# Two decode attentions on one core: the output projection in four column groups of 128, with A's part and half of B's in a loop of matmuls into one row group

## The chip, the cores and the metric

One core of one Trainium2 chip. The metric is device time in microseconds, median over runs of one kernel. The profile is of one execution on the same core.

## The reference

Two independent attention blocks, A and B, each for a single query token with a cache of 8192 positions, 32 heads of 128. Each ends in an output projection by its own wo, and the two results stand side by side.

```python
def _A_ref(x, k_cache, v_cache, wq, wo):          # B is the same with its own tensors
    B, Sq, D = x.shape                            # 1, 1, 512
    H, Dh = 32, 128
    q = (x @ wq).reshape(B, Sq, H, Dh).transpose(0, 2, 1, 3)
    scores = jnp.einsum("bhqd,bhkd->bhqk", q, k_cache) * (Dh ** -0.5)   # 8192 keys a head
    p = softmax(scores, axis=-1)
    o = jnp.einsum("bhqk,bhkd->bhqd", p, v_cache)
    return o.transpose(0, 2, 1, 3).reshape(B, Sq, H * Dh) @ wo          # 4096 x 512
...
return jnp.concatenate([a, b], axis=-1)           # [1, 1, 1024], bf16
```

## The kernel before

**Tiling.** The 64 heads are worked through in N = 16 rounds of G = 4 heads. Each head has HP = 32 of the 128 partitions, and each partition holds T = 256 consecutive positions of its head. A round's K and V are 8 MB each. `kn` holds two rounds of K (two slots), `vn` one round of V.

**One round.** VectorE multiplies K by the query, broadcast along the positions (line 280, two halves). TensorE adds up the 128 products of each position by matmuls with the identity into `rps` (lines 432 to 438: a loop of NJ = 4 steps of four matmuls, whose address comes from the register `koff`), and VectorE finishes the sum (line 308). Lines 313, 315, 476 and 478 find the maximum of each head and spread it; ScalarE takes the exponentials and their sums (line 383). Line 484 sums the denominators over the partitions. Line 492 multiplies by V: 64 matmuls of 512 columns in four column groups, that is, four strips of 32 rows of the result `acc`, which the array can work on side by side. The If at line 489 waits, in the last two rounds, for the last quarter of V, which those rounds load by itself. In the next round VectorE's `part` (lines 285 to 292) adds up the pieces of `acc`, line 442 sums them over partitions, and line 297 divides by the denominator: four columns of `oD`, one for each head.

**Start.** wq of A and B come first into `vn`. Line 405 turns x on its side, and the loop at line 409 projects the queries: eight steps, each with an If (line 410) and eight matmuls of 512 columns (line 419), both of whose operands are addressed from registers. ScalarE copies the result into `qmem` (line 372). POOL's clears (lines 170 to 180, `o2` among them) must be done before TensorE's first matmul (line 402).

**End.** In the last round, once the round before is summed up (line 442), `mid` (lines 447 to 467) projects what is ready: all 32 heads of A and B's first 16. wo stands in `kn`, A's in the first half and B's in the second. The heads' outputs are first brought into wo's row order: VectorE spreads them with a mask (line 329), a matmul sums the spread pieces (line 450), and VectorE copies the result into `o2` (line 337). `o2[:, h, :]` has two columns for each head: the head's own vector, in column 0 for A and column 1 for B, and zeros. Line 452 clears the accumulator `yps[0]`, and line 461 then adds 48 products of 512 columns, head after head round the four column groups (`k = h % G * HP`), two rows in each. VectorE copies `yps[0]` to `yc` (line 348), and line 466 adds up the four groups' rows with a selector, in fp32, into two halves of 256 columns in `yps[1]`: rows 0 and 1 hold the first half for A and B, rows 32 and 33 the second.

Only then does TensorE go on to the last round's denominators (line 484) and V (line 492). Its queue keeps the program's order, so all of this waits behind `mid`. The 16 heads of B that are left follow in pieces of wo as they land (lines 497 to 509): two matmuls of 256 columns for each head, one to each half. Line 442 for the last four heads stands before the second piece; the last piece of heads waits for line 297's division (line 503). At the end VectorE and ScalarE copy a half each (lines 352 and 386), and ScalarE's queue stores two rows of 512.

**Queues.** All large loads go through SyncE's queue in the order written (lines 222 to 233). The last ones are A's wo and B's first 16 heads, the last round's V in two pieces, and B's other heads in six pieces. Small loads of x and the store are in ScalarE's queue.

Of the kernel before, what the change touches and what calls it, by code (L numbers as in the profile page):

```python
# [8 lines left out]
BF16 = mybir.dt.bfloat16  # L9
F32 = mybir.dt.float32  # L10

P = 128
# [33 lines left out]
def bass_concat_heads__mha_block_cached__gqa_block_cached__decode_kernel(  # L46
# [18 lines left out]
    NA = 2  # L65
    H, Sk, Dh = ks[0].shape[1:]
    D = xs[0].shape[2]
    NOUT = wos[0].shape[1]
# [4 lines left out]
    G = 4  # L73
    HP = P // G
# [15 lines left out]
    WOB = [(0, 16, True), (16, 4, True), (20, 4, True), (24, 4, True), (28, 2, False), (30, 1, False),  # L90
           (31, 1, False)]
    RG = [32, 16, 4]
    NH = NOUT // 2

    with ExitStack() as st:
        ec = st.enter_context
# [2 lines left out]
        def sb(name, shape, dt):  # L99
            return ec(nc.sbuf_tensor(name, shape, dt))  # L100

        KS = T * Dh
        kn = sb("kn", [P, 2 * KS], BF16)
# [4 lines left out]

        qmem = sb("qmem", [P, N * Dh // 2], F32)
        qflat = qmem[:].bitcast(BF16)  # L110
        yc = qmem[:, 0:NOUT]
        pt = sb("pt", [P, T + W, G], BF16)
        ptf = pt[:].rearrange("p t g -> p (t g)")
        s_sb = sb("s_sb", [P, T], F32)
# [3 lines left out]
        ones_bf = sb("ones_bf", [P, P], BF16)  # L118
        ones_f = sb("ones_f", [P, P], F32)
        zrow = sb("zrow", [1, P], BF16)  # L120
        ident = sb("ident", [P, P], BF16)
        ident_f = sb("ident_f", [P, P], F32)
        sel16 = sb("sel16", [P, W, G], F32)
# [6 lines left out]
        rinv = sb("rinv", [P, G], F32)  # L130
        oD = sb("oD", [P, G + NA * H], BF16)
        zb = sb("zb", [P, 2, P], BF16)
        o2 = sb("o2", [P, NA * H, NA], BF16)
        mask = {g: sb("mask%d" % g, [P, P // g], BF16) for g in RG}
        jsel = {g: sb("jsel%d" % g, [P, g], BF16) for g in RG}
        out_sb = sb("out_sb", [NA, NOUT], BF16)

        def ps(name, shape):
            return ec(nc.psum_tensor(name, shape, F32))
# [6 lines left out]
        yps = [ps("yps%d" % i, [P, 512]) for i in range(2)]  # L146
# [3 lines left out]
        def sem(name):  # L150
            return ec(nc.semaphore(name))

        s_x, s_woa, s_v, s_v2, s_out = (sem(n) for n in ("s_x", "s_woa", "s_v", "s_v2", "s_out"))
# [4 lines left out]
        c_pool, c_sel, c_mul, c_sr, c_g, c_gm, c_self, c_st, c_o, c_rl, c_yd = (  # L158
            sem(n) for n in ("c_pool", "c_sel", "c_mul", "c_sr", "c_g", "c_gm", "c_self", "c_st", "c_o", "c_rl", "c_yd"))

        c_qa, c_nb, c_p, c_ya = (sem(n) for n in ("c_qa", "c_nb", "c_p", "c_ya"))

        c_q, c_red, c_gx, c_bc, c_pv, c_ex, c_rm, c_y = (
            sem(n) for n in ("c_q", "c_red", "c_gx", "c_bc", "c_pv", "c_ex", "c_rm", "c_y"))

        RED = NB * NJ

        @block.gpsimd
        def _(e):
# [74 lines left out]
        def _(e):  # L244
            with once(e):
# [48 lines left out]
                def outs(dst):  # L294
                    w_self()
                    w_ex()
                    e.tensor_tensor(dst, mtp[:, EX:EX + G], rinv[:], ALU.mult).then_inc(c_o, 1)  # L297
# [36 lines left out]
                def lay(i):  # L334
                    a, h0, n = todo[i]
                    e.wait_ge(c_rm, i + 1)
                    e.tensor_copy(o2[:, a * H + h0:a * H + h0 + n, a],
                                  lay_ps[i][:, 0:n]).then_inc(c_rl, 1)


# [2 lines left out]
                for i in range(len(todo)):  # L343
                    lay(i)
                    if i + 2 < len(todo):
                        spread(i + 2)
                e.wait_ge(c_y, 1)
                e.tensor_copy(yc, yps[0][:]).then_inc(c_yd, 1)
                part()
                outs(o2[:, NA * H - G:NA * H, NA - 1])  # L350
                e.wait_ge(c_y, 2)
                e.tensor_copy(out_sb[:, 0:NH], yps[1][0:NA, 0:NH]).then_inc(c_yd, 1)  # L352


        @block.scalar
        def _(e):
            with once(e):
                for a in range(NA):
                    e.dma_start(xrow[a:a + 1, :], xs[a][0]).then_inc(s_x, 16)
                w_q = _Stepped(e, c_q, 1, 1)  # L360
                w_bc = _Stepped(e, c_bc, 1, 1)
                w_nb = _Stepped(e, c_nb, 1, 1)
                w_pv = _Stepped(e, c_pv, 1, 1)
                e.wait_ge(c_pv, 1)
                e.copy(xT[:].rearrange("p (a c) -> p c a", c=C),
                       misc[:, 0:C * NA].rearrange("p (c a) -> p c a", a=NA)).then_inc(c_qa, 2)
                with e.Fori(0, N // 2) as r:
                    for j in range(2):
                        w_q()
                        for h in range(G):  # L370
                            p = slice(h * HP, (h + 1) * HP)
                            i = e.copy(qflat[p, bass.ds(r * (2 * Dh) + j * Dh, Dh)],  # L372
                                       yps[j][p, h * Dh:(h + 1) * Dh])
                        i.then_inc(c_qa, 1)
                e.wait_ge(c_pool, NPOOL)
                with e.Fori(0, N):
                    w_bc()
                    e.activation(negb[:], bmp[:, 0:G], AF.Copy, scale=-scale).then_inc(c_nb, 1)  # L378
                    w_nb()
                    w_pv()  # L380
                    for h in range(G):
                        p = slice(h * HP, (h + 1) * HP)
                        e.activation(pt[p, 0:T, h], s_sb[p, :], AF.Exp, bias=negb[p, h:h + 1], scale=scale,  # L383
                                     accum_out=rsum[p, h:h + 1]).then_inc(c_p, 4)
                e.wait_ge(c_y, 2)
                e.copy(out_sb[:, NH:NOUT], yps[1][HP:HP + NA, 0:NH]).then_inc(c_ya, 1)
                e.wait_ge(c_yd, 2)
                e.wait_ge(c_ya, 1)
                e.dma_start(out[0].rearrange("o (a n) -> (o a) n", a=NA), out_sb[:]).then_inc(s_out, 16)


        @block.tensor
        def _(e):
            with once(e):
# [9 lines left out]
                for c in range(C):  # L404
                    i = e.matmul(misc[:, c * NA:(c + 1) * NA], xrow[:, c:D:C], ident[0:NA, 0:NA],
                                 start=True, stop=True)
                i.then_inc(c_pv, 1)
                e.wait_ge(s_w[0], 16)
                with e.Fori(0, N // 2) as r:
                    with e.If(r == GA // 2):  # L410
                        e.wait_ge(s_w[1], 16)
                    a = r // (GA // 2)
                    w0 = r * (2 * G * Dh) + a * (WQ - H * Dh)
                    x0 = a * C
                    for j in range(2):
                        e.wait_ge(c_qa, by_tile)
                        e.reg_add(by_tile, by_tile, 1)
                        for c in range(C):
                            i = e.matmul(  # L419
                                yps[j][:], xT[:, bass.ds(x0 + c, 1)].broadcast_to([P, P]),  # L420
                                vn[:, bass.ds(w0 + (c * H * Dh + j * G * Dh), G * Dh)],
                                start=(c == 0), stop=(c == C - 1))
# [21 lines left out]
                def wo_rows(h):  # L444
                    return kn[:, h * NOUT:(h + 1) * NOUT]

                def mid():
                    for i, (a, h0, n) in enumerate([(0, 0, H)] + [(1, h0, n) for h0, n, rows in WOB if rows]):
                        e.wait_ge(c_rl, (1, 2, 4, 6, 8)[i])
                        e.matmul(lay_ps[i][:, 0:n], zb[:, i % 2, :], jsel[n][:], start=True,  # L450
                                 stop=True).then_inc(c_rm, 1)
                    e.matmul(yps[0][:], zrow[:], ones_bf[0:1, 0:1].broadcast_to([1, 512]), start=True,
                             stop=False, skip_group_check=True)
                    e.wait_ge(c_rl, 5)
                    for h in range(H + WOB[0][1]):
                        if h == 0:
                            e.wait_ge(s_woa, 16)
                        if h == H:
                            e.wait_ge(s_wob[0], 16)
                        k = h % G * HP  # L460
                        i = e.matmul(yps[0][k:k + NA, :], o2[:, h, :], wo_rows(h), start=False,
                                     stop=False, skip_group_check=True)
                    i.then_inc(c_y, 1)
                    e.wait_ge(c_yd, 1)
                    for b in range(2):
                        e.matmul(yps[1][b * HP:b * HP + NA, 0:NH], sel16[:, 0, 0:NA],
                                 yc[:, b * NH:(b + 1) * NH], start=True, stop=False, skip_group_check=True)

                with e.Fori(0, N) as r:
                    with e.Fori(0, NB // 2):  # L470
# [16 lines left out]
                    for g in range(NG):  # L487
# [3 lines left out]
                        k = g % G * HP  # L491
# [5 lines left out]
                for g in range(1, len(WOB)):  # L497
                    h0, n, rows = WOB[g]
                    if g == 2:
                        total_of_group()  # L500
                    e.wait_ge(s_wob[g], 16)
                    if h0 == H - G:
                        e.wait_ge(c_o, N + 1)
                    for h in range(h0, h0 + n):
                        for b in range(2):
                            m = e.matmul(yps[1][b * HP:b * HP + NA, 0:NH], o2[:, H + h, :],  # L506
                                         wo_rows(H + h)[:, b * NH:(b + 1) * NH], start=False,
                                         stop=(h == H - 1), skip_group_check=True)
                m.then_inc(c_y, 1)

# [27 lines left out]
```

## Time and profile before

| what | value |
|---|---|
| runs before, median (lowest to highest) | 666.0 us (665.41 to 666.83) |
| the profiled execution's own time | 665.7 us |
| its span | 664.2 us |
| mean granted TensorE clock | 0.784 |
| TensorE matmuls busy | 385.1 us, 58% |
| VectorE busy | 363.3 us, 55% |
| ScalarE busy | 76.0 us, 11% |
| DMA | 285.22 MB, 429 GB/s over the span |

Times in views are microseconds from the span's start. "Busy" of an engine is the union of its instructions; an engine's idle time before an instruction is put down to what released it. A name with q (PEldq, SPq) is the sequencer of that engine: address arithmetic on registers, branches and DMA issues are seen there. In a line of a group or a source line, the three numbers of a duration are the lowest, the median and the highest in ns. In a view by windows the columns are the stretch and its length, then the busy time and count of TensorE's matmuls, its weight loads, VectorE, ScalarE and POOL, then the granted clock, the DMA's share and GB/s. The clock is a share of full speed: 0.50 is half.

### The profile page before, as it was taken

The numbers are of one execution on the slowest core, as the hardware profiler recorded it, in microseconds if no ns is written. First come the engines' busy times: TensorE is split into PE (matmuls) and PEld (weight loads), VectorE is DVE, ScalarE is ACT, GpSimd is POOL, SyncE is SP. The second block draws the span as 40 slices with busy tenths as digits, with TensorE's granted clock in tenths as the row PEclk, the third lists the DMA queues.
The fourth block names the chain that finished last, engine by engine and source line by source line (L and its number), as shares of the span: only waits on it lengthen the run. The fifth ranks groups of instructions, "written<-read, shape, count | busy, mean of one in ns | idle before, by whom it ended". The sixth has DMA issues, their size and how long they took to land.

```text
span 664.2 us, 7946 instructions
## 1 busy us (share of the span) xinstructions
PE 385.1 (58%) x2398; PEld 169.4 (25%) x2398; DVE 363.3 (55%) x250; ACT 76.0 (11%) x211; POOL 2.3 (0%) x12
## 2 busy tenths in 40 slices
PE   1719392854819275481928548192854819285776
PEld 0203141322304132230413223041322304132332
DVE  1046757548292654829275482927547292754821
ACT  1710202020010202001020200102020010202020
POOL 1000000000000000000000000000000000000000
PEclk9968787786958778695877869597786959778789
DMA  9999999999999999999989999999999999989998
GB/s 379 442 442 442 442 442 391 430 442 442 442 442 399 422 442 442 442 442 442 442 387 434 442 442 442 442 442 414 406 442 442 442 442 442 434 387 458 426 413 344
DMA packets 6472, 285.22 MB, mean 429 GB/s; under 512 B 708, under 2 KB 1224, under 8 KB 1608
## 3 DMA queue, kind: packets, MB, share of 16 engines
q1 hardware_dynamic: 6464, 285.22, 99.5%
q10 hardware_dynamic: 8, 0.00, 0.0%
HBM read 285.21 MB, written 0.00 MB: 429 GB/s over the span
## 4 chain that ended last, share of the span: by engine, by line
DMA 82%; PE 15%; issue 1%; ACT 1%; SPq 0%; ACTq 0%; DVE 0%
DMA vn<-in_A_v_cache_dram 41%; DMA vn<-in_B_v_cache_dram 34%; PE acc L492 13%; DMA kn<-in_B_wo_dram 5%; PE yps L419 2%; DMA vn<-in_A_wq_dram 2%; ACT qmem L372 1%; SPq L220 0%; PE yps L506 0%; SPq L208 0%; ACTq L43 0%; ACTq L372 0%; DVE out_sb L352 0%
## 5 line engine op out<-in xcount | busy, mean ns | idle before, releaser
L280 DVE TENSOR_TENSOR kn<-kn,qmem 128x16384 bf16<-128x16384 bf16 x32 | 276.7, 8688 | 49.6 <-DMA kn<-in_A_k_cache_dram 37.1
L436 PE MATMUL rps<-kn,ident 128*128 x1024 | 236.2, 383 | 0.4
L492 PE MATMUL acc<-vn,pt 128*32 128x512 bf16 x1024 | 92.0, 537 | 153.5 <-DMA vn<-in_A_v_cache_dram 80.4
L308 DVE TENSOR_REDUCE s_sb<-rps 128x64 f32<-128x512 f32 x64 | 44.3, 692 | 166.8 <-PE rps L436 166.8
L436 PEld LDWEIGHTS rps<-kn,ident 128*128 128x128 bf16 x1024 | 96.5, 98 | 110.4 <-issue 22.3
L492 PEld LDWEIGHTS acc<-vn,pt 128*32 128x32 bf16 x1024 | 38.4, 129 | 200.6 <-issue 194.3
L378 ACT ACTIVATE negb<-bmp 128x4 f32<-128x4 f32 x16 | 2.8, 173 | 547.3 <-PE bmp L478 547.3
L383 ACT ACTIVATE pt<-s_sb,negb 32x256 bf16<-32x256 f32 x64 | 54.9, 858 | 4.3 <-ACT negb L378 3.0
L484 PE MATMUL misc<-rsum,ones_f 128*128 128x4 f32 x32 | 9.2, 358 | 56.4 <-ACT pt L383 56.4
L285 DVE TENSOR_SCALAR om<-acc,msk 128x128 f32<-128x128 f32 x16 | 5.6, 350 | 41.8 <-PE acc L492 41.8
L484 PEld LDWEIGHTS misc<-rsum,ones_f 128*128 128x128 f32 x32 | 7.8, 304 | 58.2 <-ACT pt L383 57.7
L419 PE MATMUL yps<-vn,xT 128*128 x64 | 17.4, 422 | 8.5 <-ACT qmem L372 4.4
L288 DVE SCALAR_TENSOR_TENSOR om<-acc,msk,om 128x128 f32<-128x128 f32 x48 | 16.8, 351 | 5.9
L430 PE MATMUL rps<-ones_bf,zrow 1*128 1x1 bf16 x64 | 11.0, 172 | 15.6 <-DVE kn L280 15.4
L476 PE MATMUL mtp<-ident_f,m 128*1 128x128 f32 x32 | 6.1, 270 | 22.6 <-DVE m L313 22.6
L372 ACT CAST qmem<-yps 32x128 f32 x64 | 16.4, 256 | 9.4 <-PE yps L419 8.6
L430 PEld LDWEIGHTS rps<-ones_bf,zrow 1*128 1x128 bf16 x64 | 5.8, 91 | 42.8 <-issue 42.8
L383 ACT ACTIVATION_READ_ACCUMULATOR pt<-s_sb,negb 32x1 f32 x64 | 15.9, 248 | 0.0
L419 PEld LDWEIGHTS yps<-vn,xT 128*128 x64 | 6.6, 103 | 18.9 <-issue 16.0
L478 PE MATMUL bmp<-gm,ones_f 1*128 1x4 f32 x32 | 6.1, 258 | 7.3 <-DVE gm L315 7.3
L297 DVE TENSOR_TENSOR oD<-mtp,rinv 128x4 f32 x15 | 2.4, 162 | 13.6 <-PE mtp L442 13.6
L315 DVE TENSOR_REDUCE gm<-mtp 1x4 f32<-1x128 f32 x16 | 4.5, 279 | 8.9 <-PE mtp L476 8.9
(56 smaller groups left out, 50.9 us busy)
## 6 DMA issues: line engine op xcount, KB each, us to landing
vn<-in_B_v_cache_dram SPq DMA_DIRECT2D x2, 6144.0 KB, 28.0
vn<-in_A_wq_dram SPq DMA_DIRECT2D x1, 4096.0 KB, 12.2
vn<-in_B_wq_dram SPq DMA_DIRECT2D x1, 4096.0 KB, 21.4
vn<-in_B_v_cache_dram SPq DMA_DIRECT2D x2, 2048.0 KB, 32.5
kn<-in_A_wo_dram SPq DMA_DIRECT2D x1, 4096.0 KB, 27.8
kn<-in_B_wo_dram SPq DMA_DIRECT2D x1, 2048.0 KB, 32.3
kn<-in_B_wo_dram SPq DMA_DIRECT2D x3, 512.0 KB, 34.1
kn<-in_B_wo_dram SPq DMA_DIRECT2D x1, 256.0 KB, 35.2
```

Of the source, the lines that this page charges most:

```text
L280: e.tensor_tensor(k, k, qflat[:, bass.ds(q, Dh)].unsqueeze(1).broadcast_to([P, HM, Dh]), ALU.mult).then_inc(c_mul, 2)
L288: e.scalar_tensor_tensor(om[t % 2][:], acc[:, t * Dh:(t + 1) * Dh], msk[:, t:t + 1], om[(t + 1) % 2][:], ALU.mult, ALU.add).then_inc(*((c_ ...
L308: e.tensor_reduce(s_sb[:, h * HT:(h + 1) * HT], rps[:, h % 2, :].rearrange("p (t d) -> p t d", d=DW), AX.X, ALU.add).then_inc(c_sr, 1)
L372: i = e.copy(qflat[p, bass.ds(r * (2 * Dh) + j * Dh, Dh)], yps[j][p, h * Dh:(h + 1) * Dh])
L383: e.activation(pt[p, 0:T, h], s_sb[p, :], AF.Exp, bias=negb[p, h:h + 1], scale=scale, accum_out=rsum[p, h:h + 1]).then_inc(c_p, 4)
L419: i = e.matmul(yps[j][:], xT[:, bass.ds(x0 + c, 1)].broadcast_to([P, P]), vn[:, bass.ds(w0 + (c * H * Dh + j * G * Dh), G * Dh)], start=(c ...
L430: e.matmul(rps[:, tile, 0:1], zrow[:], ones_bf[0:1, 0:1], start=True, stop=False, skip_group_check=True)
L436: m = e.matmul(ro, ident[:], src, start=False, stop=False, skip_group_check=True)
L476: e.matmul(mtp[0:1, 0:P], m1[:], ident_f[:], start=True, stop=True).then_inc(c_gx, 1)
L478: e.matmul(bmp[:, 0:G], ones_f[0:1, :], gm[:], start=True, stop=True).then_inc(c_bc, 1)
L484: e.matmul(misc[:, 0:G], ones_f[:], rsum[:], start=True, stop=True)
L492: m = e.matmul(acc[k:k + HP, :], ptf[:, g * W * G:g * W * G + HP], vn[:, g * W * Dh:(g + 1) * W * Dh], start=(g < G), stop=(g >= NG - G))
```

## The change

1. `o2` has MR = 17 columns for each head in place of 2. A's vectors stand in column 0, B's in column 16 (ST = 16).
2. The 48 products in `mid` become a loop of 12 steps with four heads in each. All go to rows 0 to 16 of `yps[0]`, one column group; both operands are addressed from the loop's register. Before, heads went round the four groups. The loop has an If for the step from which B's wo is needed. A's result is row 0 and B's row 16. The clear before it has one column in place of 512.
3. The result in `yps[1]` stands in four column groups of 128 columns (NQ) in place of two of 256: four fp32 products by the identity bring `yc` there, and each of the last 16 heads issues four matmuls of 128 columns in place of two of 256.
4. One copy of [128, 128] by VectorE takes the place of a copy by VectorE and one by ScalarE. The store takes eight rows of 128 out of `out_sb` (every 16th partition).
5. The loop raises `c_y` once in each step, and VectorE waits for 12 and 13 in place of 1 and 2; the semaphore `c_ya` is gone.

```diff
-    NH = NOUT // 2
+    NQ = NOUT // G
+    ST = HP // NA
+    MR = ST + 1
...
-        yc = qmem[:, 0:NOUT]
+        yc = qmem[0:MR, 0:NOUT]
...
-        o2 = sb("o2", [P, NA * H, NA], BF16)
+        o2 = sb("o2", [P, NA * H, MR], BF16)
+        o2f = o2[:].rearrange("p h m -> p (h m)")
...
-        out_sb = sb("out_sb", [NA, NOUT], BF16)
+        out_sb = sb("out_sb", [P, NQ], BF16)
...
+        NY = (H + WOB[0][1]) // G
...
-                    e.tensor_copy(o2[:, a * H + h0:a * H + h0 + n, a],
+                    e.tensor_copy(o2[:, a * H + h0:a * H + h0 + n, a * ST],
...
-                e.wait_ge(c_y, 1)
-                e.tensor_copy(yc, yps[0][:]).then_inc(c_yd, 1)
+                e.wait_ge(c_y, NY)
+                e.tensor_copy(yc, yps[0][0:MR, :]).then_inc(c_yd, 1)
                 part()
-                outs(o2[:, NA * H - G:NA * H, NA - 1])
-                e.wait_ge(c_y, 2)
-                e.tensor_copy(out_sb[:, 0:NH], yps[1][0:NA, 0:NH]).then_inc(c_yd, 1)
+                outs(o2[:, NA * H - G:NA * H, ST])
+                e.wait_ge(c_y, NY + 1)
+                e.tensor_copy(out_sb[:], yps[1][:, 0:NQ]).then_inc(c_yd, 1)
...
-                e.wait_ge(c_y, 2)
-                e.copy(out_sb[:, NH:NOUT], yps[1][HP:HP + NA, 0:NH]).then_inc(c_ya, 1)
                 e.wait_ge(c_yd, 2)
-                e.wait_ge(c_ya, 1)
-                e.dma_start(out[0].rearrange("o (a n) -> (o a) n", a=NA), out_sb[:]).then_inc(s_out, 16)
+                e.dma_start(out[0].rearrange("o (a b n) -> (o b) a n", a=NA, b=G),
+                            out_sb[0:P:ST, :]).then_inc(s_out, 16)
...
-                    e.matmul(yps[0][:], zrow[:], ones_bf[0:1, 0:1].broadcast_to([1, 512]), start=True,
-                             stop=False, skip_group_check=True)
+                    e.matmul(yps[0][0:MR, 0:1], zrow[:, 0:MR], ones_bf[0:1, 0:1], start=True, stop=False,
+                             skip_group_check=True)
                     e.wait_ge(c_rl, 5)
-                    for h in range(H + WOB[0][1]):
-                        if h == 0:
-                            e.wait_ge(s_woa, 16)
-                        if h == H:
+                    e.wait_ge(s_woa, 16)
+                    with e.Fori(0, (H + WOB[0][1]) // G) as i:
+                        with e.If(i == H // G):
                             e.wait_ge(s_wob[0], 16)
-                        k = h % G * HP
-                        i = e.matmul(yps[0][k:k + NA, :], o2[:, h, :], wo_rows(h), start=False,
-                                     stop=False, skip_group_check=True)
-                    i.then_inc(c_y, 1)
+                        for h in range(G):
+                            m = e.matmul(yps[0][0:MR, :], o2f[:, bass.ds(i * (G * MR) + h * MR, MR)],
+                                         kn[:, bass.ds(i * (G * NOUT) + h * NOUT, NOUT)], start=False, stop=False,
+                                         skip_group_check=True)
+                        m.then_inc(c_y, 1)
                     e.wait_ge(c_yd, 1)
-                    for b in range(2):
-                        e.matmul(yps[1][b * HP:b * HP + NA, 0:NH], sel16[:, 0, 0:NA],
-                                 yc[:, b * NH:(b + 1) * NH], start=True, stop=False, skip_group_check=True)
+                    for b in range(G):
+                        e.matmul(yps[1][b * HP:(b + 1) * HP, 0:NQ], ident_f[0:MR, 0:HP],
+                                 yc[:, b * NQ:(b + 1) * NQ], start=True, stop=False, skip_group_check=True)
...
                     for h in range(h0, h0 + n):
-                        for b in range(2):
-                            m = e.matmul(yps[1][b * HP:b * HP + NA, 0:NH], o2[:, H + h, :],
-                                         wo_rows(H + h)[:, b * NH:(b + 1) * NH], start=False,
+                        for b in range(G):
+                            m = e.matmul(yps[1][b * HP:b * HP + MR, 0:NQ], o2[:, H + h, :],
+                                         wo_rows(H + h)[:, b * NQ:(b + 1) * NQ], start=False,
                                          stop=(h == H - 1), skip_group_check=True)
```

More of the change, by code (lines that the diff above doesn't have):

```diff
@@ L159, in bass_concat_heads__mha_block_cached__gqa_block_cached__decode_kernel @@
             sem(n) for n in ("c_pool", "c_sel", "c_mul", "c_sr", "c_g", "c_gm", "c_self", "c_st", "c_o", "c_rl", "c_yd"))
-        c_qa, c_nb, c_p, c_ya = (sem(n) for n in ("c_qa", "c_nb", "c_p", "c_ya"))
+        c_qa, c_nb, c_p = (sem(n) for n in ("c_qa", "c_nb", "c_p"))
         c_q, c_red, c_gx, c_bc, c_pv, c_ex, c_rm, c_y = (
```

## The prediction

> **What bounds the kernel now.** I read the chain of waits first, then its last microseconds, then the order of TensorE's work over the last 30 us.
>
> ```profile
> DMA 82%; PE 15%; issue 1%; ACT 1%; SPq 0%; ACTq 0%; DVE 0%
> ...
> 626.38 35.17 DMA kn<-in_B_wo_dram
> 661.59 0.64 PE yps L506 x6
> ...
> 662.28 0.29 PE yps L506 x2
> 662.59 0.41 DVE out_sb L352
> ```
>
> The stream of K, V and weights fills the span, and its last piece, B's wo, lands at 626.38 + 35.17 = 661.55; only the last heads' matmuls, the copies and the store stand behind it. The edited work (lines 452 to 466) is not in this chain. So the question is how much TensorE's own line of work may grow before it ends last. The order of time on TensorE, with idle time and its releaser in brackets:
>
> ```profile
> 644.94 0.60 PE L452 MATMUL yps<-ones_bf,zrow 1*128 1x512 bf16 x1
> 645.47 4.98 PE L461 MATMUL yps<-kn,o 128*2 128x512 bf16 x48
> 651.26 0.60 PE L466 MATMUL yps<-qmem,sel 128*2 128x256 f32 x4 [0.80 <-DVE qmem L348]
> 651.79 0.39 PE L484 MATMUL misc<-rsum,ones_f 128*128 128x4 f32 x2
> 652.17 2.77 PE L492 MATMUL acc<-vn,pt 128*32 128x512 bf16 x48
> 657.06 1.05 PE L492 MATMUL acc<-vn,pt 128*32 128x512 bf16 x16 [2.12 <-DMA vn<-in_B_v_cache_dram]
> 658.27 0.60 PE L506 MATMUL yps<-kn,o 128*2 128x256 bf16 x8 [0.16 <-DMA kn<-in_B_wo_dram]
> 659.99 0.38 PE L442 MATMUL mtp<-selh,om 128*128 128x4 f32 x2 [1.12 <-DVE om L288]
> 660.30 1.14 PE L506 MATMUL yps<-kn,o 128*2 128x256 bf16 x16
> 661.59 0.96 PE L506 MATMUL yps<-kn,o 128*2 128x256 bf16 x8 [0.15 <-DMA kn<-in_B_wo_dram]
> ```
>
> The slack is 2.1 us at the wait for V's last quarter (657.06), and about 1 us more in the waits of the last heads: with all weights there, the 12 heads behind line 442 need some 1.2 us (below) from 660.30, so 661.5 to 661.7 in place of 662.57. The 48 matmuls of line 461 may therefore take about 3.1 us more than now (8.1 in place of 4.98, or 0.17 us each) before the end moves.
>
> **The 48 matmuls.** Now they go round four column groups. They take 4.98/48 = 0.104 us each; one alone lasts 631 ns, so several run at once:
>
> ```profile
> L461 PE MATMUL yps<-kn,o x48: 380/631/634, 645.5 to 650.1; 128*2 128x512 bf16 x48
> ...
> 646.50:650.00 3.50, 3.50 (x36) 1.11 (x32) 0.00 (x0) 0.00 (x0) 0.00 (x0) 0.50 1.04 449
> 650.00:651.00 1.00, 0.46 (x8) 0.00 (x0) 0.49 (x1) 0.00 (x0) 0.00 (x0) 1.00 0.00 0
> ```
>
> The number after POOL's pair is the granted clock: 0.50 while line 461 runs, 1.00 from 650.0. Four in parallel at 0.104 us are 0.43 us for one group at half clock. After the change all 48 go into one group of 17 rows, so they follow one another. What one group takes at full clock stands in the loop of line 436 (also 512 columns, one output region, four matmuls to a step with an address from a register) and in the q projection, line 419:
>
> ```profile
> 601.05 3.73 PE L436 MATMUL rps<-kn,ident 128*128 x16
> ...
> 20.54 1.90 PE L419 MATMUL yps<-vn,xT 128*128 x8 [0.71 <-ACT qmem L372]
> ```
>
> With 0.38 us for the last one, 3.73 gives 3.35/15 = 0.223 and 1.90 gives 1.52/7 = 0.217 us each. By the array alone the loop takes 4.5 us at half clock (10.5 matmuls, to 650.0) and 37.5 x 0.216 = 8.1 after that: an end at 658.3.
>
> **The loop's own instructions.** TensorE's sequencer works out addresses and branches between matmuls, and line 409's loop shows what one step costs, since it too has an If and two addresses from registers for each matmul:
>
> ```profile
> L409 PEldq ALU_OP  x1: 36/36/36, 21.8 to 21.8; - x1
> L409 PEldq COMPARE_BRANCH  x1: 218/218/218, 21.9 to 21.9; - x1
> L409 PEldq MOVE  x1: 37/37/37, 22.2 to 22.2; - x1
> ...
> L410 PEldq COMPARE_BRANCH  x1: 214/214/214, 22.3 to 22.3; - x1
> ...
> L417 PEldq FUSED_REGOPS  x3: 60/178/178, 20.2 to 22.8; - x3
> ...
> L419 PEldq FUSED_REGOPS  x7: 46/65/84, 20.4 to 21.7; - x7
> ...
> 20.16 0.39 issue
> ...
> 20.54 0.57 PEld L419 LDWEIGHTS yps<-vn,xT 128*128 x4 [1.20 <-issue]
> ...
> L436 PEldq FUSED_REGOPS  x12: 46/46/46, 601.1 to 604.0; - x12
> L432 PEldq COMPARE_BRANCH  x4: 73/208/215, 601.5 to 604.2; - x4
> ```
>
> The 0.39 us of issue holds the 178 and the 65 ns operations, which leaves some 0.06 us of gap with each. Counter, back branch, move and the If's branch are then 36 + 218 + 37 + 214 = 505 ns and four gaps, 0.75 us, which their starts confirm (21.8 to 22.3, and 0.21 more). Four weight loads in 0.57, with 0.10 for the last, start 0.157 us apart: that is a matmul whose two addresses are computed. A step of the new loop is 0.75 + 4 x 0.157 = 1.38 us, well over the 0.87 of four matmuls at full clock, so **the sequencer sets the pace** once the clock is up, and the array idles in each step. Bounds: with line 436's single 46 ns operation in each matmul (0.125 apart) 1.25 us; with the first operation of each step as dear as line 417's 178 ns, 1.38 + 0.11 and a gap or two, 1.59. I take 1.38, since lines 409 to 419 are the same shape of code. The clock stays up at such a duty, to judge by the q projection:
>
> ```profile
> 20.00:23.20 3.20, 1.93 (x9) 0.81 (x9) 0.00 (x0) 2.59 (x11) 0.00 (x0) 1.00 1.14 492
> ```
>
> TensorE was busy 60% there at 1.00. In the first steps the half clock (1.71 us for four) is slower than the sequencer, which runs ahead meanwhile; the array catches up after 650.0, so the clock matters little.
>
> [...]
>
> **The sum**, on the profiled execution. The zero matmul shrinks from 512 columns to one, yet entering the loop (two moves, the If, a first operation: 0.6 us with gaps) takes its place, so the first matmul stays at 645.5. The last step starts 11 x 1.38 later, its last matmul 0.47 after that, and ends 0.38 on: **661.5 against 650.45, +11.1 us**. All later steps are queued behind it on TensorE or wait for VectorE's copy of its result.
>
> ```profile
> 650.51 0.69 DVE L348 COPY qmem<-yps 128x512 f32<-128x512 f32 x1 [5.30 <-PE yps L461]
> 641.20 0.38 PE L476 MATMUL mtp<-ident_f,m 128*1 128x128 f32 x2 [1.41 <-DVE m L313]
> L506 PEld LDWEIGHTS yps<-kn,o x32: 79/80/84, 658.3 to 662.3; 128*2 128x2 bf16 x32
> L506 PE MATMUL yps<-kn,o x32: 270/271/273, 658.3 to 662.3; 128*2 128x256 bf16 x32
> 663.04 0.27 ACTq L389 DMA_DIRECT2D out_dram<-out_sb  x1
> L285 DVE TENSOR_SCALAR om<-acc,msk 128x128 f32<-128x128 f32 x16 | 5.6, 350 | 41.8 <-PE acc L492 41.8
> ```
>
> - Copy and line 466: the copy keeps its 512 columns whatever its rows, so 650.45 to 651.26 repeats: 662.35. Four fp32 products of 128 columns in four groups replace two of 256 (0.53 us from 651.26 to 651.79). I take 0.4; 0.3 if all go at once, 1.5 if the four stood in line at line 476's 0.38. Line 484 adds 0.38: line 492 starts at 663.1.
> - Line 492: V is there, so the wait of 2.12 us is gone. 48 in 2.77 is 2.39/11 = 0.217 for each round of four, so 64 take 15 x 0.217 + 0.38 = 3.63: 666.8, +8.7.
> - VectorE's combination, unchanged: 658.11 to 659.99 is 1.88: line 442 at 668.6; the next heads start 0.31 later. The 16 heads now issue 64 matmuls of 128 columns in place of 32 of 256. Four heads in 0.60 are (0.60 - 0.27)/3 = 0.11 us a head. Half the columns would make it 0.055, but each weight load lasts 80 ns and serves one matmul, so I take 0.11 again; the other bound is line 492's 0.217. Heads 16 to 19 lie beside VectorE's 1.88; the other 12 take 11 x 0.11 + 0.22 and no longer wait for wo (DMA, done by 662.3): 670.4, +7.8.
> - Copies and store: one copy of 128 elements in place of two of 256, 0.41 down to about 0.29 (line 285 has 0.35 for 128). Eight rows of 256 bytes in place of two of 1 KB: no row shows more rows from ScalarE's queue, so between nothing and 0.3 us, as much again as the 0.27 of issue; I take nothing. 664.2 - 662.57 - 0.12 = 1.51: the span is **671.9**.
>
> The execution's own time is 1.5 over its span (665.7 to 664.2), so **673.4 us**, 7.7 over it; the median of the runs, 666.0, is 0.3 over this execution.
>
> Free of cost: o2 grows from 128 to 1088 elements for each partition, and POOL clears it before TensorE may start.
>
> ```profile
> 1.87 0.19 POOL L179 MEMSET o<- 128x128 bf16 x1
> 2.01 0.96 POOL L180 MEMSET pt<- 128x1040 bf16 x1
> 9.43 0.26 PE L405 MATMUL misc<-ident,xrow 2*128 2x2 bf16 x4 [9.43 <-DMA xrow<-in_B_x_dram]
> ```
>
> That is some 0.8 us more, up to 3.8, where x arrives at 9.4; without that cover it would cost 0.8. No load's issue is moved or gated by the change.
>
> **Rivals.**
> - *The array sets the pace* (register work and branches hidden, by the queue ahead of the array): end of loop 658.3, 3.2 us earlier, so 670.2 us. For it: line 436's loop loses little to its own branch (0.223 against 0.217). Against: that loop has one branch and one short operation, no If.
> - *The clock stays at half* through the loop, if short gaps count as idle: 48 x 0.427 ends at 666.2, and line 492 at 0.43 a round adds 3.2: about 681 us. The q projection's 1.00 at 60% duty speaks against it.
> - *Not slower*: matmuls of one group overlap, so that the loop takes under 8.1 us, 0.17 each. Then the wait for V and wo's landing absorb it, the bound stays with the DMA, and the smaller copy leaves 665.6 us. It decides at 0.17; lines 436 and 419 show 0.217 to 0.223 and no overlap within a group. [...]
>
> **How the numbers follow.** Forecast 0.72, the array's pace 0.16, half clock 0.06, not slower 0.04, and 0.02 for ends between. The step's bounds give 672.0 (1.25) to 675.7 (1.59), at 11 us for each us of it; the smaller terms (fp32 -0.1 to +1.1, heads -0.6 to +1.2, store 0 to +0.3) widen that to about 671.3 to 677. With the array's case the range is 669.5 to 677.2. A difference of 0.2% (1.3 us) is about what a measurement of this kernel tells from none: faster 0.02, same 0.03, slower 0.95.
>
> **What would show it.** In the changed kernel's profile: the loop's matmuls from 645.5 to about 661.5 with gaps in each step, and branches of some 0.21 us; no wait for V before line 492's last 16; the chain's end on TensorE and no longer on wo; line 492 at about 663. A loop of under 8 us, or one whose matmuls run at 0.22 without gaps, would prove the pace wrong; heads at 0.2 us each, or a store over 1.5 us, would move the tail.

## The result, and the profile after

The changed kernel takes 673.84 us in the median (673.56 to 674.53), the kernel before 666.12 in the same comparison: a ratio of 1.012, with a 95% interval of 1.0108 to 1.0133. It is slower by 1.2%. The profiled execution took 673.56 us, with a span of 672.2. One run of a later experiment (no If: 686.09 us, at a clock of 0.619) was in a slower state and is not counted in its median.

First the shares of the chain of waits of the changed kernel, then the end of that chain (start, duration, what).

```profile
DMA 76%; PE 20%; issue 2%; DVE 1%; ACT 1%; ACTq 0%; DVEq 0%
```

```profile
645.48 8.01 PE yps L462 x24
653.48 0.38 issue
653.86 1.03 PE yps L462 x4
...
660.85 1.04 PE yps L462 x4
661.92 0.69 DVE qmem L352
...
663.39 3.59 PE acc L494 x64
...
669.22 0.85 PE yps L508 x48
670.10 0.29 DVE out_sb L356
```

The DMA's share fell from 82% to 76%, and wo's landing is gone from the end. From 645 us on the chain runs through TensorE: the loop (line 462 now), VectorE's copy, V (494), the last sums and heads (508). Within the loop "issue" (0.38 us in the view) appears between groups of four matmuls: the profile shows nothing there that TensorE waits for, which leaves its own sequencer. The first six steps, 645.48 to 653.49, show no gap: half clock (0.50 from 645.0 to 650.5, with the array busy 5.09 of the 5.50 us) makes the array the slower part at first, as the prediction said, so the gaps that it expected in each step stand in the last six alone.

TensorE's order of time in the changed kernel:

```profile
655.21 1.03 PE L462 MATMUL yps<-kn,o 128*17 x4 [0.33 <-issue]
...
662.65 0.42 PE L468 MATMUL yps<-qmem,ident_f 17*32 17x128 f32 x8 [0.77 <-DVE qmem L352]
...
663.32 3.64 PE L494 MATMUL acc<-vn,pt 128*32 128x512 bf16 x64
...
668.83 0.39 PE L444 MATMUL mtp<-selh,om 128*128 128x4 f32 x2 [1.66 <-DVE om L292]
669.15 0.90 PE L508 MATMUL yps<-kn,o 128*17 128x128 bf16 x48
```

All 64 matmuls of V now run in one stretch: the 2.12 us that TensorE waited before its last 16 are gone, and so are the waits for wo. That slack has been used up.

What one step of the loop holds beside its matmuls (lowest, median, highest in ns; lines 458 and 459 are the loop and its If):

```profile
L458 PEldq MOVE  x13: 29/37/38, 644.9 to 660.4; - x13
L458 PEldq ALU_OP  x12: 36/36/36, 646.0 to 661.4; - x12
L458 PEldq COMPARE_BRANCH  x12: 79/215/217, 646.1 to 661.5; - x12
...
L459 PEldq COMPARE_BRANCH  x13: 78/214/214, 645.1 to 660.4; - x13
...
L462 PEldq FUSED_REGOPS  x48: 74/74/84, 645.3 to 661.2; - x48
```

Two branches of 0.21 us and four address operations of 74 ns stand in each step. From 653.86 to 660.85 are five steps: 1.40 us each. The loop takes from 645.48 to 660.85 + 1.03 = 661.88, 16.40 us where it took 4.98.

### The profile page after: what moved, and what is told of

Same layout as the page of the kernel before. It is cut to its first block, busy times and chain, and to the rows that moved or that the text cites. A ratio compares the mean times of both kernels' runs of the same rounds, so it can differ in the third digit from the quotient of the medians.

```text
span 672.2 us, 8114 instructions
## 1 busy us (share of the span) xinstructions
PE 390.5 (58%) x2434; PEld 171.9 (26%) x2434; DVE 362.9 (54%) x250; ACT 75.7 (11%) x210; POOL 3.1 (0%) x12
## 4 chain that ended last, share of the span: by engine, by line
DMA 76%; PE 20%; issue 2%; DVE 1%; ACT 1%; ACTq 0%; DVEq 0%
DMA vn<-in_A_v_cache_dram 41%; DMA vn<-in_B_v_cache_dram 33%; PE acc L494 13%; PE rps L438 2%; PE yps L462 2%; PE yps L421 2%; DMA vn<-in_A_wq_dram 2%; ACT qmem L376 1%; DVE om L292 0%; PE yps L508 0%; DVE zb L333 0%; PE mtp L444 0%; DVE s_sb L312 0%; DVE qmem L352 0%; DVE o L341 0%
## 5 line engine op out<-in xcount | busy, mean ns | idle before, releaser
L494 PE MATMUL acc<-vn,pt 128*32 128x512 bf16 x1024 | 89.6, 527 | 152.9 <-DMA vn<-in_A_v_cache_dram 81.6
L376 ACT CAST qmem<-yps 32x128 f32 x64 | 16.4, 257 | 9.9 <-PE yps L421 9.2
L462 PE MATMUL yps<-kn,o 128*17 x48 | 14.2, 445 | 2.6 <-issue 2.6
```

The lines of the kernel that those rows point to most:

```text
L376: i = e.copy(qflat[p, bass.ds(r * (2 * Dh) + j * Dh, Dh)], yps[j][p, h * Dh:(h + 1) * Dh])
L462: m = e.matmul(yps[0][0:MR, :], o2f[:, bass.ds(i * (G * MR) + h * MR, MR)], kn[:, bass.ds(i * (G * NOUT) + h * NOUT, NOUT)], start=False, ...
L494: m = e.matmul(acc[k:k + HP, :], ptf[:, g * W * G:g * W * G + HP], vn[:, g * W * Dh:(g + 1) * W * Dh], start=(g < G), stop=(g >= NG - G))
```

## The experiments

Three things changed at once: the order of the products (one column group, the title's "row group"), the loop, and the end (four groups of 128, one copy, eight rows). The runs take them apart. The theory was the prediction's: most of the loss is one group in series, and the sequencer's pace adds some 3 us to it.

**The products written out, still in one group.**

```diff
-                    with e.Fori(0, (H + WOB[0][1]) // G) as i:
-                        with e.If(i == H // G):
+                    for h in range(H + WOB[0][1]):
+                        if h == H:
                             e.wait_ge(s_wob[0], 16)
...
+                        m = e.matmul(yps[0][0:MR, :], o2[:, h, :], wo_rows(h), start=False, ...)
```

> The changed kernel with its 48 products written out, fixed addresses, still all in one column group (rows 0 to 16). Theory (the sequencer's 1.40 us a step sets the loop's end, some 3.2 us over what one group needs in series): the products run without gaps, about 0.427 us each at half clock and 0.216 at full, end near 658.6 instead of 661.9, and the time is 670.5 us (669.9 to 671.1). Rival, series in one group is all of the loss: 673.8 unchanged. Rival, the loop is all of the loss: 666 to 667.

Measured: 670.45 us (670.25 to 671.07), ratio to before 1.0071 (1.0054 to 1.0088). On TensorE:

```profile
646.03 12.22 PE L461 MATMUL yps<-kn,o 128*17 128x512 bf16 x48
659.02 0.42 PE L467 MATMUL yps<-qmem,ident_f 17*32 17x128 f32 x8 [0.77 <-DVE qmem L352]
```

No gaps: 12.22 us against 16.40 in the loop. So the theory holds: the series in one group costs 7.2 us of TensorE's time over before, and the loop's own instructions another 4.2. That the time met its 670.5 is in part luck: these products started at 646.03, 0.55 us later than in the changed kernel, which is part of why the two medians lie 3.4 apart and not 4.2.

**The products written out, in four groups again, with the new end.** The output row is `h % G * HP`, and a selector sums the groups.

> As the run before, but the 48 products go round four column groups again (17 rows in each, summed by a selector as before the change); the end (four groups of 128, one copy, eight rows stored) stays as changed. Theory: the products end near 650.4, the waits for V and for wo are back, and only the dearer store is left (its issue 0.65 against 0.27 us): 666.4 us (665.9 to 667.0). Rival, the new end costs something itself (17 columns, 64 matmuls for 16 heads, one copy): 667.5 or more.

Measured: 667.34 us (666.80 to 668.05), ratio 1.0021 (1.0011 to 1.003). The loss of the products is gone, as expected, but the time is 0.9 over what I expected, above its range and just below the rival's 667.5. TensorE's order of time shows where:

```profile
646.11 5.25 PE L464 MATMUL yps<-kn,o 128*17 128x512 bf16 x48
...
658.07 1.90 PE L496 MATMUL acc<-vn,pt 128*32 128x512 bf16 x16 [2.14 <-DMA vn<-in_B_v_cache_dram]
...
662.37 1.46 PE L510 MATMUL yps<-kn,o 128*17 128x128 bf16 x48
```

The wait for V is back, but V came 1 us later than before (658.07 against 657.06), and the 16 matmuls behind it took 1.90 us in place of 1.05. The windows of this kernel, before and behind that wait, show a clock at half from 658 on:

```profile
653.00:656.00 3.00, 2.77 (x48) 1.35 (x48) 0.00 (x0) 0.00 (x0) 0.00 (x0) 1.00 0.98 419
658.00:660.00 2.00, 1.93 (x28) 0.98 (x32) 0.00 (x0) 0.00 (x0) 0.00 (x0) 0.50 1.02 402
```

The slow end need not be the new end's doing: two runs below, both with the old end, which differ in nothing but their stores, take 0.61 and 1.03 us for the same eight matmuls of 256 columns in this stretch. The last of the experiments returns to V's lateness.

**A second If in each step.**

```diff
                         with e.If(i == H // G):
                             e.wait_ge(s_wob[0], 16)
+                        with e.If(i == H // G + 1):
+                            e.wait_ge(s_wob[0], 16)
```

> The changed kernel with a second If in each of the 12 steps, whose body is a wait that is long met. Theory (sequencer's pace): each step longer by one branch, one move and their gaps, 0.37 us, so 1.77 us a step and 12 x 0.37 = 4.4 us more: 678.2 us (677.0 to 679.0). Rival, the array sets the pace and hides it: 673.8 unchanged, or under 675.

Measured: 677.72 us (676.78 to 677.94). The steps on TensorE, and the added branch:

```profile
652.23 1.03 PE L464 MATMUL yps<-kn,o 128*17 x4 [0.36 <-issue]
...
663.91 1.03 PE L464 MATMUL yps<-kn,o 128*17 x4 [0.61 <-issue]
```

```profile
L461 PEldq COMPARE_BRANCH  x13: 72/208/213, 645.3 to 663.5; - x13
```

Seven steps in 11.68 us are 1.67 each, 0.27 more: the branch of 0.208 with one gap and no move (I had put 0.37). The span grew by 3.1 us to 675.3, which is 0.26 for each of 12 steps. An array that set the pace would have hidden it. The time met the range by luck: 4.4 us were expected for the steps and 3.1 came, and the rest of the 3.9 lies outside the span (in the profiled execution 2.5 us stand between span and time, where the changed kernel had 1.4).

**Half the columns in each product.** The second operand is cut to its first 256 columns.

> The changed kernel with each product of the loop over the first 256 of its 512 columns alone; the other half of A's and of B's first 16 heads' share is left out. Theory (sequencer's pace): the steps stay at 1.40 us, the loop ends at 661.8 or 0.1 earlier, 673.7 us (673.0 to 674.0). Rival (array's pace): half the columns take half the time, the loop ends near 653.5 and the time falls to 666 to 667.

Measured: 677.08 us (675.98 to 678.21): neither of the two. On TensorE:

```profile
653.93 1.02 PE L462 MATMUL yps<-kn,o 128*17 x4 [0.38 <-issue]
...
660.92 1.02 PE L462 MATMUL yps<-kn,o 128*17 x4 [0.33 <-issue]
...
663.81 6.29 PE L494 MATMUL acc<-vn,pt 128*32 128x512 bf16 x64
```

The steps stayed at (660.92 - 653.93)/5 = 1.40 us, and the loop ended at 661.94, where it ended before. The array's time did not fall as I had assumed, since the clock stayed at half: four matmuls of 256 columns took 1.02 us, as long as four of 512 at full clock. But at some 0.21 us each the array alone would still have been done near 656, so the sequencer's pace is borne out. What I had missed comes after the loop: V took 6.29 us in place of 3.64. The windows (granted clock ahead of the DMA's share) show why, first of the changed kernel, then of this one:

```profile
645.00:650.50 5.50, 5.09 (x13) 1.64 (x13) 0.17 (x1) 1.35 (x4) 0.00 (x0) 0.50 0.99 429
655.00:661.00 6.00, 4.26 (x17) 1.48 (x17) 0.00 (x0) 0.00 (x0) 0.00 (x0) 1.00 0.98 380
```

```profile
651.00:657.00 6.00, 4.29 (x18) 1.62 (x18) 0.00 (x0) 0.00 (x0) 0.00 (x0) 0.50 0.97 408
664.00:669.00 5.00, 5.00 (x52) 1.82 (x48) 0.00 (x0) 0.00 (x0) 0.00 (x0) 0.50 0.00 0
```

At the same busy share, 4.26 and 4.29 of 6.00, one kernel stays at full clock and the other at half. Ahead of these stretches the two differ: the changed kernel's first steps had the array busy 5.09 of 5.50 us at 0.50, while this loop never filled it (4.20 of the 6.00 us from 645 to 651, at 0.53). But V kept the array busy here without a gap from 664 to 669, and the clock was still at half. What brings it up is not shown: no run changed the first steps alone.

**No If, and eight heads in a step.** The first cuts the loop in two around the wait; the second has `range(2 * G)` in six steps.

> The changed kernel with its loop cut in two (8 steps, the wait for B's wo, 4 steps), so that no step has an If. Theory: a step of the sequencer falls by the If's branch, move and gaps, 0.37 us, from 1.40 to 1.03; the lead that it gains while the clock is at half (0.43 us a matmul) then lasts to the end, and the array, not the sequencer, sets the end, as with the products written out: about 670.6 us (670.2 to 671.3). Rival, the loop's cost lies in the address work of each matmul and not in the branches: 673 to 674.

> The changed kernel with eight heads in each of six steps (one If, one back branch for eight matmuls). Theory: a step is 0.78 + 8 x 0.154 = 2.0 us, 0.25 a matmul, and with the lead from the half clock the array sets the end: about 670.6 us (670.2 to 671.3). Rival (address work): 6 x 2.8, no change, 673.8.

Measured: with eight heads 670.51 us (670.01 to 671.21), ratio 1.0073 (1.0057 to 1.0088), as expected. Without the If it is 673.36 us (673.33 to 673.53), ratio 1.0112 (1.0093 to 1.013), which misses the expectation and falls into the rival's 673 to 674. Its span of 668.7 speaks for the theory even so: the two loops end at 658.4, with no gap left for the address work.

```profile
645.94 12.04 PE L462 MATMUL yps<-kn,o 128*17 x48 [0.41 <-issue]
```

```profile
645.19 9.45 PE L460 MATMUL yps<-kn,o 128*17 x32
654.48 3.91 PE L467 MATMUL yps<-kn,o 128*17 x16
...
659.16 0.42 PE L473 MATMUL yps<-qmem,ident_f 17*32 17x128 f32 x8 [0.77 <-DVE qmem L352]
```

The first line is eight heads in a step, the others are the two loops. The gaps are gone in both. The 4.8 us between the span and the time of the two loops (1.4 in the changed kernel) lie outside what the spans show. Behind the span, from 668.8 to 674, the DMA queues hold an instruction fetch of 0.02 MB (q8), which the changed kernel does not have there; the smaller one (q14) it has too:

```profile
q8 instruction: 1, 0.02, 1.4%
q14 instruction: 1, 0.01, 0.6%
```

The same fetch stands after the spans of the second If and of the loop with the old end, whose profiled executions took 2.5 and 2.75 us over their spans. The traced executions of the ten other kernels took 1.4 to 1.7 over theirs; in four of them (before, changed, the first experiment, eight heads) the queues behind the span show the smaller fetch alone. Some runs of these ten, without a trace, took up to 2.7. What calls for it, and whether it is the whole of the difference, stays open.

**The loop with the end as before, and four groups with the end as before.** Two halves of 256 columns, two copies, rows 0 and 16 stored as two rows of 512.

```diff
-                    for b in range(G):
-                        e.matmul(yps[1][b * HP:(b + 1) * HP, 0:NQ], ident_f[0:MR, 0:HP], ...)
+                    for b in range(2):
+                        e.matmul(yps[1][b * HP:(b + 1) * HP, 0:NH], ident_f[0:MR, 0:HP], ...)
...
+                e.dma_start(out[0].rearrange("o (a n) -> (o a) n", a=NA), out_sb[0:MR:ST, :])
```

> The changed kernel (loop, one group) with the end as before: two halves of 256 columns, two copies, two rows of 512 stored. Theory: 12 heads behind the last sum at 0.11 instead of 0.056 us each cost 0.65, the store's issue at 0.27 instead of 0.65 us gives back 0.4 to 0.5: 673.9 us (673.3 to 674.5), and the store's issue shows 0.27. Rival, the eight rows cost nothing or the old end is dearer: 674.5 or more.

> Products written out in four column groups, as in the second experiment, and the end as before the change; left of the change are the 17 columns and the clear of one column. Theory: the second experiment's 1.65 us over before came from the eight-row store (0.5) and from a clock that fell to half at the wait for V; with two rows it is 666.2 us (665.6 to 666.8). Rival, the 17 columns or the selector cost: 667.3.

Measured: the loop with the old end 675.94 us (674.71 to 676.25), 2.0 over what I expected and in the rival's range; four groups with the old end 666.72 (666.01 to 667.31), ratio 1.0011 (1.0002 to 1.002), inside the range. The lines of the first on TensorE and ScalarE's queue:

```profile
669.52 1.48 PE L511 MATMUL yps<-kn,o 128*17 128x256 bf16 x24
```

```profile
671.50 0.72 ACTq L394 DMA_DIRECT2D out_dram<-out_sb  x1
```

The 24 matmuls of 256 columns take 1.48 us where 48 of 128 took 0.90, as expected (0.6). But the store of two rows still takes 0.72 us to issue, not 0.27. So the number of rows alone is not what makes it dear, and nothing is given back. The rest of the 2 us is 0.3 of a later start of the loop and up to 1.4 more outside the span. The second on TensorE:

```profile
644.84 5.07 PE L467 MATMUL yps<-kn,o 128*17 128x512 bf16 x48
...
656.71 1.05 PE L499 MATMUL acc<-vn,pt 128*32 128x512 bf16 x16 [2.12 <-DMA vn<-in_B_v_cache_dram]
```

Products and wait for V are as before the change. Its hit is in part luck: it was to gain 0.5 us by a cheaper store, and that store takes 0.71 us too, as the next runs show.

**Rows side by side.** The store's rows 0 to 7 in the changed kernel; rows 0 and 1 in the kernel with four groups and the old end.

```diff
-                            out_sb[0:P:ST, :]).then_inc(s_out, 16)
+                            out_sb[0:NA * G, :]).then_inc(s_out, 16)
```

> The changed kernel, with the store taking rows 0 to 7 of the result in place of every 16th row (of the output only A's first 128 columns are then right; the rest is left out). If the step over partitions makes the store's issue dear, it falls from 0.65 us to about 0.3, and the span by 0.3 to 0.4 us; if the number of rows does, it stays at 0.65.

> The kernel with four groups and the old end, which stores rows 0 and 16 (issue 0.71 us), with rows 0 and 1 stored instead; B's result is left out. If the step over partitions is what costs, the issue is 0.27 us as before the change and the span falls by 0.4; if not, 0.7.

Measured, in one run each: 673.29 and 666.26 us. The issues on ScalarE's queue, in this order:

```profile
L390 ACTq DMA_DIRECT2D out_dram<-out_sb x1: 757/757/757, 670.0 to 670.0; - x1
```

```profile
L397 ACTq DMA_DIRECT2D out_dram<-out_sb x1: 274/274/274, 663.4 to 663.4; - x1
```

and, for the second, the kernel it was made from, with rows 0 and 16:

```profile
L397 ACTq DMA_DIRECT2D out_dram<-out_sb x1: 713/713/713, 662.7 to 662.7; - x1
```

Two rows side by side take 0.27 us, rows 0 and 16 take 0.71. Eight rows side by side take 0.76. So the step over partitions is dear for two rows, but without it eight rows are no cheaper; in the output these eight still go to places that are not in order. The one cheap form (0.27 us, here and before the change) is dense on both sides. Which side counts for eight rows was not tried. The span of the first is 671.9, 0.3 under the changed kernel's, and its loop also began 0.25 earlier. The span of the second, 664.6, is no shorter than the 664.5 of the kernel that it was made from: its last 24 matmuls took longer, as TensorE's order of time shows (2.26 us from 659.95 in that kernel), so the span does not tell. The eight of these matmuls before them took longer too: 1.03 us from 657.95, and 0.61 from 657.92 in that kernel.

```profile
660.20 2.73 PE L513 MATMUL yps<-kn,o 128*17 128x256 bf16 x24
```

**One group written out, with the old end.** It has 36 matmuls and their weight loads fewer on TensorE than the first experiment (2398 in place of 2434). It is to tell why V was late in the first two.

> Products written out in one column group, with the end as before the change: 64 instructions fewer on TensorE than in the first experiment. There, and in the second, a 16 KB instruction fetch ran at 75 us, and the first V landed at 82 us instead of 80.7 to 81. Theory: the longer program caused the fetch, and the fetch made the whole stream 1 us late; without it the first V lands at 80.7 to 81.1, the last sum starts 1 us earlier, and with heads 0.6 us dearer the time is 669.9 us (669.2 to 670.8). Rival, the 1 us is a difference between executions: V at 82 here too, or at 82 without a fetch, and 671 us.

Measured: 669.37 us (669.24 to 669.61), ratio 1.0056 (1.0039 to 1.0072). The first V's transfer in the chain of the first experiment, and then of this run:

```profile
35.45 46.65 DMA vn<-in_A_v_cache_dram
```

```profile
35.73 44.86 DMA vn<-in_A_v_cache_dram
```

The DMA queues of the first experiment from 60 to 90 us:

```profile
q1 hardware_dynamic: 239, 13.57, 104.5%
q8 instruction: 1, 0.02, 0.2%
```

V landed at 82.1 there and at 80.6 here, and this run has no such fetch. 0.2% of 16 engines over 30 us is about 1 us of one engine's time. How a fetch of that length could hold V back by 1 us is not shown. The first V lands at 82.1 and 81.9 in the two kernels with the fetch and at 80.6 to 81.05 in eight others, so the theory holds as far as one trace each goes. Further on it is less clear: the products start at 646.0 and 646.1 in those two, and at 644.7 to 645.9 in the others.

No version beat the kernel before. With the products in four groups and the old end, the time is 0.1% over it (0.02% to 0.2%).

## Why the prediction was right

The predicted time was 673.4, the measured median 673.84 and this execution 673.56. Step by step, in us of the span:

| step | predicted | measured |
|---|---|---|
| first matmul of the loop | 645.5 | 645.48 |
| a step | 1.38 | 1.40 |
| end of the loop | 661.5 | 661.88 |
| fp32 products (line 468) | 662.35 | 662.65 |
| V (line 494) | 663.1 | 663.32 |
| last sum (line 444) | 668.6 | 668.83 |
| end of the last heads | 670.4 | 669.15 + 0.90 = 670.05 |
| end of the span | 671.9 | 672.2 |

**The sequencer's pace** was the step that could have gone either way, and the runs show it from three sides: a dearer step lengthens the loop by as much (second If), half the columns in each product do not shorten it (half columns), and fewer branches for each matmul make the gaps vanish (eight heads). The array's case, which had 0.16, was priced at 670.2; where the array does set the pace, the measured times are 670.45 and 670.51. I had put the array's loop at 12.8 us and it took 12.0 to 12.2, and the sequencer's at 16.0 where it took 16.4, so the sequencer's share was 4.2 and not 3.2.

**The branches** were as dear as the rows of line 409's loop had them: in the changed kernel 214 and 215 ns in the median (lines 459 and 458). The back branch at the end of the last step, which is not taken, took 79 ns, and the If's own 78 in the one step that enters its body.

**The clock** stayed at 1.00 through the gaps, as forecast (4.26 of 6.00 us busy). But the ground for it was too short: the one window of the q projection showed a clock that stayed up (1.00 with 1.93 of 3.20 us busy), and not what raises it. With half the columns the same busy share went with 0.50 through the loop from 651 on (4.29 of 6.00). So the rival of half clock, at 0.06, was nearer than its chance says.

**No overlap within a group**: the steps' four matmuls take 1.03 us, 0.38 of it the last one's, so 0.217 us each at full clock. The quickest 48 in one group, written out, took 12.01 us, where the rival needed under 8.1. The two kernels in four groups confirm that the DMA's end is the bound once the products are quick (5.25 and 5.07 us): TensorE again waits 2.14 and 2.12 us for V.

**Two small terms were wrong and cancel.** "Each weight load lasts 80 ns and serves one matmul, so I take 0.11 again": the 12 heads took 0.90 us, (0.90 - 0.22)/11 = 0.062 each, while one weight load lasts 0.09. The 48 weight loads are busy 0.72 us together, where 48 times 0.09 would be 4.3, so several run at once, and the half of the columns is gained: 0.5 us less. "No row shows more rows from ScalarE's queue ... I take nothing": the issue took 0.65 in place of 0.27, and the stretch from the last heads to the span's end 672.2 - 670.05 = 2.15 in place of 1.51, 0.6 us more and past the bound of 0.3. That the sum still came out within 0.3 us is in part luck.

The range is not summed evenly: the upper bounds named for it add up to 675.7 + 1.1 + 1.2 + 0.3 = 678.3, where it stops at 677. The measured time lies far inside either.

Clearing the larger `o2` was hidden, as said: POOL was done at 3.8 us and x arrived at 9.3.

## What to carry to other kernels

A hardware loop around a few matmuls had its own price here (16.40 us for 48, in place of 12.22 written out), which the trace shows on the sequencer's rows: add its branches, counter and address operations for one step and compare them with the array's time for that step; put more matmuls in a step before giving up the loop (eight in place of four took 12.04 us, without the gaps). Products with few output rows were quicker in several column groups: 48 took 4.0 to 5.3 us in four groups, and no less than 12.0 in one. TensorE, off the critical path, had a slack here, estimated from its waits at 3.1 us, and the change was not free beyond it: 11.4 us more in the loop made the span 8.0 longer.

## What the runs showed of the hardware

- One busy share went with two clocks: with the array busy 71% of the time by the records it stayed at 1.00 in one kernel, where a nearly full stretch had gone before (5.09 of 5.50 us), and at 0.50 in another without one (4.20 of 6.00), where the next stage took 2.65 us more (V at 0.50 in 6.29 in place of 3.64).
- A store's issue on ScalarE's queue took 0.27 us for two dense rows of 1 KB, 0.71 for rows 16 partitions apart, and 0.65 to 0.76 for eight rows.
- An instruction fetch of 0.02 MB in mid-stream went with a transfer that landed 0.8 to 1.5 us later than in eight other traces. After the span, such a fetch went with times 2.5 to 4.8 us over the span, in place of 1.4 to 1.7 in the other traced executions.
